# A delta-rule layer with a rational feed-forward on one core: the denominator's product on GpSimd, chunk scalars on VectorE, and a new written-out order

## The chip, the cores and the metric

The kernel runs on one core of a Trainium2 chip. A core has TensorE (PE; its weight loads are shown apart as PEld), VectorE (DVE), ScalarE (ACT), GpSimd (POOL) and SyncE (SP, which here only issues transfers). Each engine works through its own list of instructions in order and waits on semaphores. The metric is the device time of one execution in microseconds (us), the median of several.

## The reference

Two parts follow each other. The first is a delta-rule recurrence for each of 4 x 8 heads over 768 time steps with head size 48; the second is a feed-forward layer over the 3072 tokens with a rational function between two matrix products (384 to 2048 to 384).

```python
k_n = k / (np.linalg.norm(k, axis=-1, keepdims=True) + 1e-06)
for t in range(S):
    y[:, :, t] = einsum('bhd,bhde->bhe', q[:, :, t], state)
    v_old = einsum('bhde,bhd->bhe', state, kt)
    state = state + bt[..., None, None] * einsum('bhd,bhe->bhde', kt, vt - v_old)
x = y.transpose(0, 2, 1, 3).reshape(B * S, H * D)
h = x @ w_in
P = a[0] + a[1] * h + a[2] * h * h + a[3] * h * h * h
Q = 1.0 + abs(b[0]) * abs(h) + abs(b[1]) * h * h
out = (P / (Q + 1e-06)) @ w_out
```

`w_in` and `w_out` arrive as 64-bit floats; everything else is 32-bit.

## The kernel before

The sequence is cut into 12 chunks of 64 steps. Within a chunk the recurrence is solved with matrix products: keys are normalized and transposed, their products make a triangular system whose 16x16 blocks are inverted on VectorE (`inverse`), and the rest is solved in four rounds that go from TensorE to ScalarE and VectorE and back (`solve`). State and outputs follow. This is called the delta work below. Values are held as a pair of 16-bit halves, so each product is three passes of matmuls.

The feed-forward of a chunk has 256 tokens and is cut into 8 units of 256 hidden features, so there are 96 units. A unit is 18 matmuls into `ph` (`hidden`, L864), the rational function on 128x512 values, and 12 matmuls that add to `po` (`accumulate`, L931). The rational function: `numerator` makes z = |ph * B1| (ScalarE, L884), u = A3 * ph + a2 (ScalarE, L885), w = (z + B0) * ph (VectorE, L888) and |w| (ScalarE, L890). `cubic` makes u into the numerator but for its constant (VectorE, L896 and L898). `quotient` takes Ln and Exp of the denominator (ScalarE, L904 and L906), makes the first half of the result (VectorE, L910), a correction (VectorE, L913 and L915; L913 writes into the `ph` of the next unit) and its product with r (GpSimd, L917). The 128x512 buffers `mx` rotate over three, `ph` over two.

Each chunk needs factors that scale its 8 units: `scalar_steps` works them out on values of one column (128x1) with 14 calls of a small helper `affine` on ScalarE (L815), around three reciprocals on VectorE. It is called 13 times, twice for the first chunk (half of the weights each). `scales` makes the factors of queries and values with four small operations on ScalarE (L655 to L658), and `scaled` multiplies the queries by theirs on GpSimd (L228). At the start, block-diagonal buffers are set to zero (L185), the weights are brought in and split into halves, and the delta work of the first chunks runs beside it.

Nothing is left to a scheduler: `PLACES` gives every step of every stage (a step ends at a `yield`) a place in one order of 2996 places, and each engine gets its instructions in that order. Units of one chunk are interleaved with delta work of a later chunk; four units are under way at once, as a rule. After the last delta work only units are left.

Of the kernel before, what the change touches and what calls it, by code (L numbers as in the profile page):

```python
# [11 lines left out]
F32 = mybir.dt.float32  # L12
BF16 = mybir.dt.bfloat16
U32 = mybir.dt.uint32
AF = mybir.ActivationFunctionType
# [21 lines left out]
def kernel(  # L37
# [12 lines left out]
    nc = tc.nc  # L50
# [67 lines left out]
    coef = cpool.tile([P, 12], F32, name="coef")  # L118
    bblk = cpool.tile([P, NCH, 16], F32, name="bblk")
# [11 lines left out]
    def constants(_):  # L131
# [7 lines left out]
        for t in wide.values():  # L139
            nc.vector.memset(t[:, :, :, D:], 0.0)  # L140
        nc.gpsimd.memset(consts[:, 0:1], -15.0 * LN2)
# [23 lines left out]
        nc.scalar.activation(coef[:, 6:12], coef[:, 0:6], AF.Abs)  # L165
        nc.gpsimd.tensor_scalar(bblk, bblk, 1.0 / 256.0, 0.0, op0=ALU.mult, op1=ALU.add)

    filled = {}

    def zeros(nm):  # L170
        def stage(i):
# [8 lines left out]
            if nm == "rows":  # L180
                t = kn_b[i][:, :, :, :, D:DP]
            else:
                t = wt_b[i] if nm == "wt" else diag[nm][i]
            eng = nc.vector if nm in ("k", "w", "e", "rows") else nc.gpsimd
# [45 lines left out]
    def total(src, n, nm, pool=ps_f, tag="a"):  # L230
        pf = pool.tile([P, NPAIR * 512 if pool is ps_f else n], F32, tag=tag, name="pf" + nm)[:, :n]
        nc.tensor.matmul(pf, ones, src, start=True, stop=True)
        return pf
# [18 lines left out]
    NU = NF // 2  # L252
    GROUPS = ((0, NU // 2), (NU // 2, NU))
# [10 lines left out]
    def tables(g):  # L264
# [19 lines left out]
        pt = total(io, hi - lo, f"o{lo}", ps_f, "a")  # L284
# [347 lines left out]
    def scales(c):  # L632
# [31 lines left out]
    def queries_transposed(c):  # L664
        d = info[c]
        qt = d["qt"]
        scaled(qt[..., :D], d["sq"])
# [134 lines left out]
    def scalar_steps(c, lo=0, hi=NU):  # L802
# [7 lines left out]
        gm, rk, ikap, hm, top_, low, one, lin = (kp[:, i : i + 1] for i in range(8))  # L810
# [3 lines left out]
        def affine(dst, x, by, plus=0.0):  # L814
            nc.scalar.activation(dst, x, AF.Identity, scale=by, bias=plus)  # L815
# [8 lines left out]
        nc.vector.reciprocal(kp[:, 5:7], kp[:, 5:7])  # L824
        yield
        affine(lin, hm, m1)
        affine(top_, top_, hm)
        affine(top_, top_, hm)
        affine(lin, lin, one, m0)
        affine(gm, top_, low, lin)  # L830
# [9 lines left out]
        affine(ikap, rk, rk)  # L840
        affine(sf[:, 1:2], rk, rk)
        affine(sf[:, 3:4], sf[:, 2:3], ikap)
        affine(sf[:, 4:6], sf[:, 2:4], sf[:, 2:3])
# [7 lines left out]
    unit = {}  # L851
# [4 lines left out]
    def hidden(n):  # L856
        c, f2 = divmod(n, NU)
        x = toks[c]["x"]
        ph = ps_h.tile([P, 2, TG], F32, tag="h", name=f"ph_{n}")
# [12 lines left out]
        unit[n] = {"ph": ph}  # L872

    def numerator(n):
# [3 lines left out]
        A3, B1, A1, B0, A0, Q0 = (toks[c]["m"][:, i, f2 : f2 + 1] for i in range(6))  # L878
        ph = d["ph"]

# [3 lines left out]
        nc.scalar.activation(z, ph, AF.Abs, scale=B1)  # L884
# [15 lines left out]
    def quotient(n):  # L900
# [16 lines left out]
        nc.gpsimd.tensor_mul(g[:, 1], u, r)  # L917

    def accumulate(n):
# [26 lines left out]
        for p in PAIRS:  # L946
            if lo == 0:
# [5 lines left out]
        if hi == NU:  # L953
            yield
            for b in range(2):
                dst = out[2 * b * S : (2 * b + 2) * S].rearrange("(p t) e -> t p e", p=NPAIR)
                nc.sync.dma_start(out=dst[c * C : (c + 1) * C], in_=ob[b * C : (b + 1) * C])
# [4 lines left out]
        "zero_img": (  # L962
            (0, 76),
        ),
        "weights_in": (
# [981 lines left out]
```

## Time and profile before

| | |
|---|---|
| median of 3 runs | 764.49 us (762.56 to 769.67) |
| profiled execution | 765.28 us, span 763.6 us |
| busy in the span | DVE 691.9 us (91%), ACT 661.1 (87%), PE 629.3 (82%), POOL 311.7 (41%) |
| mean granted TensorE clock | 0.939 of full speed |
| moved by DMA | 84.35 MB |

The span runs from the first to the last instruction; the execution's time is 1.7 us more. Busy shares are averages: the kernel has a stretch in which weights come in and the first chunks are worked, a long stretch of units and delta work side by side, and an end with units alone. A matmul's end is modelled, so that a group of matmuls that stands alone counts with some tail that a group with a follower doesn't have.

### The profile page before, as it was taken

Reading aid. Unit: us, or ns where it says so; the run is one execution under the profiler, and the core shown is the slowest. Engines: PE = TensorE matmul, PEld = TensorE weight load, DVE = VectorE, ACT = ScalarE, POOL = GpSimd, SP = SyncE. Lnnn points to the kernel's source line nnn. Section 1 sums busy time; section 2 is a strip of 40 time slices with the busy share of each in tenths; the row PEclk is TensorE's granted clock in tenths of the full one; section 3 lists DMA queues with packets and bytes.
Section 4 is the critical chain, followed back from the end, with each engine's and each line's share of the span. In section 5 each row is a group of like instructions: output and inputs, shape, how many; then the busy total and the mean of one; then the engine's idle time right before and its main releaser. Section 6 shows DMA issues by size and latency. Waiting matters only on the chain.

```text
span 763.6 us, 23465 instructions
## 1 busy us (share of the span) xinstructions
PE 629.3 (82%) x9520; PEld 506.6 (66%) x9520; DVE 691.9 (91%) x1288; ACT 661.1 (87%) x1301; POOL 311.7 (41%) x321
## 2 busy tenths in 40 slices
PE   1321455886898999898998999999989999999986
PEld 1221455675677788686776787787778877777753
DVE  6789988867898999898998999999989999999995
ACT  4685998978898999798997999999989996899883
POOL 6742262533344265154342463354542432323222
PEclk9955786999799999899999999999999999999999
DMA  9699999778737675678464777685755832600000
GB/s 215 194 213 196 191 174 149 119 130 129 134 73 124 88 117 98 109 124 127 89 115 81 131 118 119 108 131 87 139 81 103 138 58 36 109 1 23 1 21 22
DMA packets 358412, 84.35 MB, mean 110 GB/s; under 512 B 349856, under 2 KB 352928, under 8 KB 358304
## 3 DMA queue, kind: packets, MB, share of 16 engines
q1 hardware_dynamic: 356128, 81.69, 61.0%
q8 instruction: 75, 1.23, 0.7%
q10 hardware_dynamic: 2176, 1.17, 0.5%
q14 instruction: 33, 0.27, 0.1%
HBM read 34.70 MB, written 13.65 MB: 63 GB/s over the span
## 4 chain that ended last, share of the span: by engine, by line
DVE 32%; ACT 25%; PE 20%; DMA 10%; issue 5%; SPq 3%; POOL 2%; ACTq 0%; DVEq 0%; POOLq 0%
PE ph L864 7%; PE po L931 5%; DVE mx L888 3%; ACT mx L885 3%; DVE ph L913 3%; ACT mx L884 3%; DVE mx L915 3%; DVE mx L896 3%; DVE mg L910 3%; DVE mx L898 3%; ACT kp L815 2%; DVE w_out L311 2%; PE pu L396 2%; ACT mx L904 2%; ACT mx L890 2%
## 5 line engine op out<-in xcount | busy, mean ns | idle before, releaser
L917 POOL TENSOR_TENSOR mg<-mx 128x512 f16<-128x512 f32 x96 | 129.7, 1351 | 277.2 <-DVE mx L915 167.5
L931 PE MATMUL po<-w_out,mg 128*128 128x384 f16 x1152 | 214.5, 329 | 4.3 <-POOL mg L917 2.4
L864 PE MATMUL ph<-xT,w_in 128*128 128x256 f16 x1728 | 205.1, 273 | 10.9 <-DVE mx L915 9.3
L864 PEld LDWEIGHTS <-w_in 128*128 128x128 f16 x1728 | 165.6, 98 | 41.0 <-DVE mx L915 9.3
L931 PEld LDWEIGHTS <-mg 128*128 128x128 f16 x1152 | 109.5, 99 | 65.8 <-POOL mg L917 3.1
L910 DVE SCALAR_TENSOR_TENSOR mg<-mx,msc 128x512 f16<-128x512 f32 x96 | 73.3, 764 | 2.7 <-ACT mx L906 2.6
L884 ACT ACTIVATE mx<-ph,msc 128x512 f32<-128x512 f32 x96 | 65.2, 679 | 12.0 <-PE ph L864 10.1
L913 DVE SCALAR_TENSOR_TENSOR ph<-mx,msc,mg 128x512 f32<-128x512 f32 x96 | 73.7, 768 | 1.5
L885 ACT ACTIVATE mx<-ph,coef,msc 128x512 f32<-128x512 f32 x96 | 74.1, 772 | 0.0
L888 DVE SCALAR_TENSOR_TENSOR mx<-mx,msc,ph 128x512 f32<-128x512 f32 x96 | 70.7, 737 | 1.9 <-issue 1.1
L915 DVE SCALAR_TENSOR_TENSOR mx<-mx,msc,ph 128x512 f32<-128x512 f32 x96 | 71.1, 741 | 1.3
L898 DVE SCALAR_TENSOR_TENSOR mx<-mx,msc,ph 128x512 f32<-128x512 f32 x96 | 70.8, 738 | 0.7
L904 ACT ACTIVATE mx<-mx,msc 128x512 f32<-128x512 f32 x96 | 69.3, 722 | 1.1
L890 ACT ACTIVATE mx<-mx 128x512 f32<-128x512 f32 x96 | 60.3, 628 | 10.7 <-DVE mx L888 10.4
L396 PEld LDWEIGHTS <-kbd 128*128 128x128 f16 x1680 | 57.6, 102 | 16.9 <-DVE sw L328 7.3
L896 DVE TENSOR_TENSOR mx<-ph,mx 128x512 f32<-128x512 f32 x96 | 65.4, 681 | 0.4 <-issue 0.2
L396 PEld LDWEIGHTS <-ebd 128*128 128x128 f16 x1728 | 51.2, 98 | 15.6 <-issue 11.4
L396 PE MATMUL pu<-z,ebd 128*128 128x48 f16 x1728 | 52.0, 186 | 11.4 <-DVE z L217 10.1
L906 ACT ACTIVATE mx<-mx 128x512 f32<-128x512 f32 x96 | 60.1, 628 | 1.1
L396 PEld LDWEIGHTS <-wbd 128*128 128x128 f16 x1152 | 33.2, 98 | 40.4 <-issue 38.7
L213 POOL TENSOR_TENSOR mm<-m,mm 128x512 f16<-128x512 f32 x24 | 31.6, 1328 | 34.4 <-ACT mm L207 28.1
L217 DVE SCALAR_TENSOR_TENSOR z<-pu,zmask,z 128x768 f16<-128x768 f32 x36 | 36.4, 1011 | 5.7 <-ACT z L215 5.7
(196 smaller groups left out, 1194.0 us busy)
## 6 DMA issues: line engine op xcount, KB each, us to landing
wsi<-in_moe_w_in_dram SPq DMA_DIRECT2D x8, 768.0 KB, 6.5
wso<-in_moe_w_out_dram SPq DMA_DIRECT2D x8, 768.0 KB, 6.5
gd<-g SPq DMA_DIRECT2D x24, 256.0 KB, 4.6
mbd<-mm SPq DMA_DIRECT2D x24, 256.0 KB, 5.3
wc<-img SPq DMA_DIRECT2D x24, 256.0 KB, 5.1
wbd<-wc SPq DMA_DIRECT2D x24, 256.0 KB, 5.0
knbd<-kn SPq DMA_DIRECT2D x44, 128.0 KB, 4.1
kw<-in_k_dram SPq DMA_DIRECT2D x48, 96.0 KB, 3.3
```

The source lines that it names most:

```text
L396: nc.tensor.matmul(dst[p][:, h], head(bd, lp, p * H + h), head(rt, rp, p * H + h), start=start and n == 0 and h == 0, stop=stop and n == l ...
L864: nc.tensor.matmul(ph[:, i], w_in[:, f2, wp, cc, i * P : (i + 1) * P], x[:, xp, cc], start=k == 0, stop=k == 3 * NCC - 1,)
L884: nc.scalar.activation(z, ph, AF.Abs, scale=B1)
L885: nc.scalar.activation(u, ph, AF.Identity, scale=A3, bias=a2)
L888: nc.vector.scalar_tensor_tensor(out=w, in0=z, scalar=B0, in1=ph, op0=ALU.add, op1=ALU.mult)
L896: nc.vector.tensor_mul(u, ph, u)
L898: nc.vector.scalar_tensor_tensor(out=u, in0=u, scalar=A1, in1=ph, op0=ALU.add, op1=ALU.mult)
L910: nc.vector.scalar_tensor_tensor(out=g[:, 0], in0=u, scalar=A0, in1=r, op0=ALU.add, op1=ALU.mult)
L913: nc.vector.scalar_tensor_tensor(out=t, in0=w, scalar=Q0, in1=g[:, 0], op0=ALU.add, op1=ALU.mult)
L915: nc.vector.scalar_tensor_tensor(out=u, in0=u, scalar=A0, in1=t, op0=ALU.add, op1=ALU.subtract)
L917: nc.gpsimd.tensor_mul(g[:, 1], u, r)
L931: nc.tensor.matmul(po[p], g[:, gp, i, p * P : (p + 1) * P], w_out[:, f2, wp, i], start=f2 == lo and i == 0 and k == 0, stop=f2 == hi - 1 a ...
```

## The change

For all units but the last two, |w| is made in another way: z = |ph| (a constant scale in place of a per-partition one), then w = B1 * z + B0 on ScalarE with scale and bias by partition, then w = w * z on GpSimd. VectorE's L888 and ScalarE's L890 fall away there. `hidden` and `numerator` have one more `yield` each, so there are 3188 places.

`scalar_steps` goes to VectorE: one operation on five columns makes five of the factors, and nine more operations do the rest. Three of the four small operations of `scales` are left, on VectorE. The queries' scale goes from GpSimd to ScalarE. The four zero fills of `kbd` (two), `wbd` and `ebd` go from VectorE to ScalarE. The `ph` of the last four units are put in banks of two other pools; the last two units' last product is on VectorE in place of GpSimd; of the very last output one half is copied by VectorE and its transfer is issued from ScalarE's queue. Every place in `PLACES` is new.

```diff
     def numerator(n):
-        nc.scalar.activation(z, ph, AF.Abs, scale=B1)
+        on_pool = f2 in POOL_UNITS and n < NCH * NU - 2
+        nc.scalar.activation(z, ph, AF.Abs, scale=1.0 if on_pool else col(1))
+        yield
         nc.scalar.activation(u, ph, AF.Identity, scale=A3, bias=a2)
         yield
-        nc.vector.scalar_tensor_tensor(out=w, in0=z, scalar=B0, in1=ph, op0=ALU.add, op1=ALU.mult)
-        yield
-        nc.scalar.activation(w, w, AF.Abs)
+        if on_pool:
+            nc.scalar.activation(w, z, AF.Identity, scale=B1, bias=B0)
+            yield
+            nc.gpsimd.tensor_mul(w, w, z)
+        else:
...
     def hidden(n):
-        ph = ps_h.tile([P, 2, TG], F32, tag="h", name=f"ph_{n}")
+        if n < N - 4:
+            ph = ps_h.tile([P, 2, TG], F32, tag="h", name=f"ph_{n}")
+        else:
+            if n % 2 == 0:
+                last[0] = (ps_f if n == N - 4 else ps_c).tile([P, 2, 2, TG], F32, tag="a", name=f"ph_{n}")
+            ph = last[0][:, n % 2]
...
+            if i == 0:
+                yield
     def quotient(n):
-        nc.gpsimd.tensor_mul(g[:, 1], u, r)
+        (nc.gpsimd if n < NCH * NU - 2 else nc.vector).tensor_mul(g[:, 1], u, r)
     def scalar_steps(c, lo=0, hi=NU):
-        affine(hm, wn, gm)
-        affine(top_, hm, m3, m2)
-        affine(low, hm, b1, b0)
-        affine(one, hm, b0, 1.0)
-        affine(low, low, hm, 1.0)
...
+        nc.vector.tensor_mul(hm, wn, gm)
+        nc.vector.scalar_tensor_tensor(out=kp[:, 4:9], in0=coef[:, 7:12], scalar=hm, in1=plus, op0=mult, op1=add)
+        nc.vector.tensor_scalar(low, low, hm, 1.0, op0=mult, op1=add)
...
+        nc.vector.tensor_scalar(top_, top_, hm, hm, op0=mult, op1=mult)
+        nc.vector.tensor_scalar(lin, lin, one, m0, op0=mult, op1=add)
+        nc.vector.scalar_tensor_tensor(out=gm, in0=top_, scalar=low, in1=lin, op0=mult, op1=add)
...
+        nc.vector.tensor_mul(ikap, rk, rk)
+        nc.vector.tensor_mul(sf[:, 1:2], rk, rk)
+        nc.vector.tensor_mul(sf[:, 3:4], sf[:, 2:3], ikap)
+        nc.vector.tensor_scalar_mul(sf[:, 4:6], sf[:, 2:4], sf[:, 2:3])
     def scales(c):
-        nc.scalar.copy(sc[:, 4:5], sc[:, 3:4])
-        nc.scalar.activation(sc[:, 6:7], sc[:, 3:4], AF.Copy, scale=1.0 / 16.0)
-        nc.scalar.activation(sc[:, 5:6], sc[:, 2:3], AF.Copy, scale=sc[:, 6:7])
-        nc.scalar.activation(sc[:, 6:7], sc[:, 3:4], AF.Copy, scale=1.0 / 256.0)
+        nc.vector.tensor_scalar(sc[:, 5:6], sc[:, 3:4], sc[:, 2:3], 1.0 / 16.0, op0=ALU.mult, op1=ALU.mult)
+        nc.vector.tensor_scalar_mul(sc[:, 6:7], sc[:, 3:4], 1.0 / 256.0)
+        nc.vector.tensor_copy(sc[:, 4:5], sc[:, 3:4])
     def queries_transposed(c):
-        scaled(qt[..., :D], d["sq"])
+        nc.scalar.activation(qt[..., :D], qt[..., :D], AF.Copy, scale=d["sq"])
     def zeros(nm):
+            if nm in ('k', 'w', 'e'):
+                whole = t.bitcast(F32).rearrange(FLAT[nm])
+                nc.scalar.activation(whole, consts[:, 0:1].broadcast_to(list(whole.shape)), AF.Copy, scale=0.0)
     def accumulate(n):
+            if p and n == N - 1:
+                nc.vector.tensor_scalar_mul(ob[:, p], po[p], ikap)
...
+                queue = nc.scalar if b and n == N - 1 else nc.sync
+                queue.dma_start(out=dst[c * C : (c + 1) * C], in_=ob[b * C : (b + 1) * C])
     PLACES = {
...
```

## Rows read from the trace of the kernel before

**Rows 1.** Busy time by stretch of the span (stretch in us, its length, then for each engine the busy us and in brackets the instructions; then the mean granted TensorE clock, the DMA engines' share and GB/s).

```profile
0.00:200.00 200.00, 98.92 (x1751) 84.10 (x1752) 163.07 (x338) 156.94 (x327) 88.38 (x110) 0.80 0.88 170
200.00:250.00 50.00, 46.93 (x669) 37.32 (x666) 46.49 (x89) 46.40 (x95) 23.46 (x25) 0.97 0.62 106
250.00:700.00 450.00, 430.06 (x6723) 348.05 (x6721) 428.30 (x777) 412.92 (x800) 181.57 (x173) 0.99 0.59 98
700.00:750.00 50.00, 47.00 (x350) 33.73 (x350) 49.29 (x81) 42.59 (x81) 15.36 (x12) 1.00 0.04 9
...
sum 764.00, PE 629.31 PEld 506.64 DVE 691.90 ACT 661.13 POOL 311.74; mean PE 125.86 PEld 101.33 DVE 138.38 ACT 132.23 POOL 62.35
```

The engines in it stand in the order PE, PEld, DVE, ACT, POOL.

**Rows 2.** The page's chain of work that ended last: shares of the span by engine.

```profile
DVE 32%; ACT 25%; PE 20%; DMA 10%; issue 5%; SPq 3%; POOL 2%; ACTq 0%; DVEq 0%; POOLq 0%
```

**Rows 3.** The second matrix product alone (L931) in the long stretch and in the end: PE busy us with the number of matmuls, 12 of which make a unit.

```profile
250.00:700.00 450.00, 155.59 (x834) 78.49 (x832) 0.99 0.59 98
700.00:750.00 50.00, 25.02 (x144) 14.01 (x144) 1.00 0.04 9
```

**Rows 4.** Groups of instructions by line, each shape apart: VectorE's six operations of a unit (count | busy us, mean ns of one | idle before them and who ended it).

```profile
L888 DVE SCALAR_TENSOR_TENSOR mx<-mx,msc,ph 128x512 f32<-128x512 f32 x96 | 70.7, 737 | 1.9 <-issue 1.1 <-ACT mx L885 0.7
L896 DVE TENSOR_TENSOR mx<-ph,mx 128x512 f32<-128x512 f32 x96 | 65.4, 681 | 0.4 <-issue 0.2
L898 DVE SCALAR_TENSOR_TENSOR mx<-mx,msc,ph 128x512 f32<-128x512 f32 x96 | 70.8, 738 | 0.7
L910 DVE SCALAR_TENSOR_TENSOR mg<-mx,msc 128x512 f16<-128x512 f32 x96 | 73.3, 764 | 2.7 <-ACT mx L906 2.6
L913 DVE SCALAR_TENSOR_TENSOR ph<-mx,msc,mg 128x512 f32<-128x512 f32 x96 | 73.7, 768 | 1.5
L915 DVE SCALAR_TENSOR_TENSOR mx<-mx,msc,ph 128x512 f32<-128x512 f32 x96 | 71.1, 741 | 1.3
```

**Rows 5.** The same view: ScalarE's five operations of a unit. L890 and L906 take no factor by partition, L904 takes one, L884 one (from PSUM), L885 two (from PSUM).

```profile
L884 ACT ACTIVATE mx<-ph,msc 128x512 f32<-128x512 f32 x96 | 65.2, 679 | 12.0 <-PE ph L864 10.1 <-DVE msc L847 0.7 <-DVE mg L910 0.5
L885 ACT ACTIVATE mx<-ph,coef,msc 128x512 f32<-128x512 f32 x96 | 74.1, 772 | 0.0
L890 ACT ACTIVATE mx<-mx 128x512 f32<-128x512 f32 x96 | 60.3, 628 | 10.7 <-DVE mx L888 10.4
L904 ACT ACTIVATE mx<-mx,msc 128x512 f32<-128x512 f32 x96 | 69.3, 722 | 1.1
L906 ACT ACTIVATE mx<-mx 128x512 f32<-128x512 f32 x96 | 60.1, 628 | 1.1
```

**Rows 6.** The same view: GpSimd's product of a unit.

```profile
L917 POOL TENSOR_TENSOR mg<-mx 128x512 f16<-128x512 f32 x96 | 129.7, 1351 | 277.2 <-DVE mx L915 167.5 <-ACT mx L904 18.4 <-PE pu L396 10.5
```

**Rows 7.** All of the helper `affine` (L815) over the whole span: ACT busy us and count.

```profile
0.00:764.00 764.00, 48.08 (x182) 0.94 0.62 110
```

**Rows 8.** Groups by line: small operations of one to four columns, on ScalarE (two of the four in `scales`) and on VectorE (one and two factors by partition).

```profile
L655 ACT COPY sc<-sc 128x1 f32<-128x1 f32 x12 | 2.3, 188 | 0.6 <-DVE sc L236 0.6
L657 ACT ACTIVATE sc<-sc 128x1 f32<-128x1 f32 x12 | 3.5, 295 | 0.4
L648 DVE TENSOR_SCALAR sc<-sc,sc 128x1 f32<-128x1 f32 x11 | 2.4, 214 | 0.4
L274 DVE TENSOR_SCALAR tab<-tab,coef 128x4 f32<-128x4 f32 x2 | 0.5, 246 | 0.1
```

**Rows 9.** Groups by line: the zero fills that move, the queries' scale, and a ScalarE operation of the scale's size with one factor by partition.

```profile
L185 DVE MEMSET kbd<- 128x2048 f32 x2 | 3.5, 1765 | 0.8 <-issue 0.8
L185 DVE MEMSET wbd<- 128x2048 f32 x1 | 1.8, 1765 | 1.3 <-PEq L1933 1.3
L185 DVE MEMSET ebd<- 128x2048 f32 x1 | 1.8, 1765 | 0.4 <-issue 0.4
L228 POOL TENSOR_SCALAR qw<-qw,sc 128x768 f32<-128x768 f32 x12 | 12.3, 1023 | 18.4 <-DVE sc L236 14.4 <-DMA wc<-img 3.2 <-DVE msc L847 0.6
L215 ACT ACTIVATE sh<-S,sc 128x768 f16<-128x768 f32 x11 | 10.2, 929 | 0.0
```

**Rows 10.** The chain in order of time in a part of the long stretch (start us, us, what): a unit's two matrix products with matmuls ahead of them and behind.

```profile
322.24 1.95 PE po L931 x12
...
325.40 1.97 PE ph L864 x18
```

**Rows 11.** Instructions in order of time near the end (start us, us, engine, line).

```profile
709.55 2.13 PE L864 MATMUL ph<-xT,w_in 128*128 128x256 f16 x18
709.63 1.28 POOL L917 TENSOR_TENSOR mg<-mx 128x512 f16<-128x512 f32 x1 [3.16 <-DVE mx L915]
...
710.65 0.81 DVE L910 SCALAR_TENSOR_TENSOR mg<-mx,msc 128x512 f16<-128x512 f32 x1
```

**Rows 12.** Instructions in order of time in the long stretch.

```profile
344.34 1.52 DVE L913 SCALAR_TENSOR_TENSOR ph<-mx,msc,mg 128x512 f32<-128x512 f32 x1
344.38 0.93 POOL L213 TENSOR_TENSOR rr<-v,rr 128x384 f16<-128x384 f32 x1 [1.55 <-ACT rr L207]
```

**Rows 13.** Instructions in order of time at the very end.

```profile
753.46 2.97 POOL L917 TENSOR_TENSOR mg<-mx 128x512 f16<-128x512 f32 x2 [3.48 <-DVE mx L915]
...
757.90 1.05 ACT L948 ACTIVATE ob<-po,kp 128x384 f32<-128x384 f32 x2 [6.65 <-PE po L931]
758.98 1.25 SPq L957 DMA_DIRECT2D out_dram<-ob  x2
```

More of the change, by code (lines that the diff above doesn't have):

```diff
@@ L848, in scalar_steps @@
         d["ikap"][lo] = hi, ikap
-    unit = {}
+    N = NCH * NU
+    unit, last = {}, {}
     acc = {}
@@ new lines @@
+            (805, 822),
+            (1090, 1098),
+            (1329, 1356),
+            (1535, 1567),
+            (1802, 1825),
+            (2027, 2091),
+            (2278, 2320),
+            (2541, 2580),
+            (2736, 2748),
+        ),
+        "hidden": (
+            (397, 439),
+            (412, 414),
+            (454, 465),
+            (536, 537),
+            (566, 579),
+            (632, 647),
+            (663, 669),
+            (709, 710),
+            (732, 737),
+            (754, 758),
+            (781, 782),
+            (797, 799),
+            (847, 848),
+            (874, 881),
+            (913, 918),
+            (937, 945),
+            (977, 978),
+            (1003, 1004),
+            (1040, 1041),
+            (1059, 1071),
+            (1086, 1087),
+            (1111, 1112),
+            (1140, 1141),
+            (1180, 1185),
+            (1206, 1220),
+            (1256, 1257),
+            (1260, 1263),
+            (1306, 1307),
+            (1338, 1344),
+            (1374, 1376),
+            (1405, 1406),
+            (1437, 1438),
+            (1471, 1478),
+            (1494, 1498),
+            (1524, 1527),
+            (1551, 1557),
+            (1582, 1594),
+            (1597, 1617),
+            (1643, 1644),
+            (1685, 1686),
+            (1709, 1718),
+            (1738, 1739),
+            (1760, 1761),
+            (1790, 1810),
+            (1817, 1826),
+            (1853, 1868),
+            (1901, 1902),
+            (1933, 1938),
+            (1963, 1964),
+            (1996, 1997),
+            (2017, 2029),
+            (2045, 2050),
+            (2080, 2081),
+            (2110, 2115),
+            (2125, 2139),
+            (2168, 2169),
+            (2197, 2214),
+            (2218, 2222),
+            (2255, 2270),
+            (2296, 2298),
+            (2315, 2316),
+            (2345, 2346),
+            (2372, 2378),
+            (2393, 2397),
+            (2429, 2430),
+            (2463, 2464),
+            (2488, 2500),
+            (2513, 2521),
+            (2534, 2543),
+            (2562, 2565),
+            (2593, 2595),
+            (2622, 2625),
+            (2675, 2682),
+            (2694, 2695),
+            (2712, 2713),
+            (2737, 2738),
+            (2762, 2772),
+            (2778, 2789),
+            (2813, 2820),
+            (2831, 2837),
+            (2857, 2859),
+            (2875, 2882),
+            (2899, 2903),
+            (2920, 2922),
+            (2932, 2933),
+            (2950, 2956),
+            (2986, 2987),
+            (3002, 3005),
+            (3030, 3032),
+            (3047, 3048),
+            (3056, 3058),
+            (3086, 3087),
+            (3053, 3098),
+            (3100, 3103),
+            (3126, 3129),
+            (3132, 3135),
+        ),
```

1474 lines of the change are left out of this document (685 added, 789 removed), and 177 rows, old and new, of tables (FLAT, PLACES).

## The prediction

> **What bounds the kernel now.** I read busy time by stretch first [rows 1], because the kernel has stretches with different limits. In the first 200 us no engine is near full: PE 98.9 of 200, DVE 163.1, ACT 156.9, with DMA at 0.88. From 250 to 700 us three engines are nearly full at once: PE 430.1 of 450 (95.6%), DVE 428.3 (95.2%), ACT 412.9 (91.8%); POOL has 181.6 (40%). From 700 to 750 us, with almost no delta work left, it is DVE: 49.3 of 50 (98.6%). The chain of waits says the same, being spread over DVE 32%, ACT 25% and PE 20% [rows 2]: no one engine holds it. The long stretch counts 834 / 12 = 69.5 units, 6.47 us each, or 8.7 chunks of 51.8 us; the end counts 144 / 12 = 12 units in 50 us, 4.17 us each [rows 3]. So relieving DVE alone gains in the long stretch only until PE is the limit, and PE's work isn't touched.
>
> **The change part by part, in the long stretch.**
>
> The denominator. DVE loses L888: 69.5 x 0.737 = 51.2 us [rows 4]. ACT loses L890 (0.628) and gets an operation from SBUF with two factors by partition, which no row shows. One factor costs L904 - L906 = 94 ns, so I take 628 + 2 x 94 = 816 ns; the bounds are 722 (one factor, L904) and 772 + 94 = 866. The z operation loses its factor: 679 - 94 = 585 ns. Net 816 - 628 - 94 = +94 ns a unit, 6.5 us in the stretch [rows 5]. POOL gets a product of 128x512 with 32-bit output. The nearest row, L917, has the same shape with 16-bit output: 1.35 us [rows 6]; I take that, with 0.93 (a shorter product, [rows 12]) and 2.7 (twice L917) as ends. That is 69.5 x 1.35 = 93.8 us.
>
> The chunk scalars. ACT loses 48.1 / 13 = 3.7 us a chunk [rows 7] and four operations of 188 to 295 ns, 0.9 us [rows 8]: 8.7 x 4.6 = 40 us. DVE gets 10 and 3 operations of one to five columns at 0.15 to 0.25, I take 0.2 (214 for one column, 246 for four, less some overlap) [rows 8]: 2.6 us a chunk, 22.6 us.
>
> The queries' scale. POOL loses 1.02 us a chunk, ACT gets 0.93 (its row of that size with one factor) [rows 9]: -8.9 and +8.1 us.
>
> Sums for the 450 us: DVE 428.3 - 51.2 + 22.6 = 399.7 (89%); ACT 412.9 + 6.5 - 40 + 8.1 = 387.5 (86%); POOL 181.6 + 93.8 - 8.9 = 266.5 (59%); PE stays at 430.1 (96%). **PE becomes the limit.** How full can a limiting engine be? DVE reached 98.6% in the end [rows 1], but with simpler work. At 98.6% PE would need 436 us (-14), at today's 95.6% 450 (0). A part of PE's busy time is the modelled tail of groups that stand alone: 18 matmuls of `hidden` count 2.13 us alone [rows 11] and 1.97 with a follower [rows 10]. A denser PE sheds some of that: if each unit's 18 did, 69.5 x 0.16 = 11 us more, which makes the far end -25. I take PE at 97.5% (441) with a third of the 11 us shed: -13 us. The 50 us before it (PE 46.9, DVE 46.5) go the same way: -1.5.
>
> The first 200 us. Four fills leave DVE, 4 x 1.765 = 7.1 us, for ACT, where I reckon 1.87 each (628 ns for 512 elements, and (929 - 722) / 256 = 0.81 ns for each further one) [rows 5, 9]. ACT has 43 us of room, DVE 37. If all four were on the path it would be -7, if they now hold up ACT's own path +7.5. The order of the delta work and the transfers is new and not to be read from rows; I take -2 with those ends.
>
> The end. A unit takes 4.17 us at DVE's pace (sum of the six: 4.43, less overlap). Without L888 DVE has 3.5, and PE's 1.97 + 1.95 = 3.92 [rows 10] is next. At 4.0 the 12 units give -2; the ends are 0 and -3. The last four units' own banks take away a wait of `hidden` for the `ph` two units before, which PE's pace covers anyway: nothing. Behind the last unit: the last products on DVE take 0.76 in place of GpSimd's 2.97 for two, of which PE waits for some 0.8; two output copies side by side, 1.05 to 0.6; two issues on two queues, 1.25 to 0.6 [rows 13]: -1.9.
>
> Sum: -2 - 1.5 - 13 - 2 - 1.9 = -20.4, from a span of 763.6 to 743.2; the execution's time lies 1.7 above it, 744.9, and the profiled execution lay 0.8 above the median of the runs shown: **744 us**, -2.7%.
>
> **What is queued behind the new waits.** Ln (L904) now waits for GpSimd's product, and behind it in ACT's list stand Exp and the next units' z and u, on which PE's second product and `ph`'s release hang. On GpSimd the product stands among the delta work's halves and L917.
>
> **The rivals.**
>
> *Ln waits for GpSimd (slower).* Before, ACT waited 10.7 us in all for DVE at L890 and 1.1 at L904 [rows 5]. ACT will have 450 - 387.5 = 62.5 us of room in the stretch, 0.90 us a unit. If Ln stands on average more than 0.90 us idle for a product of 1.35 us or more, ACT's list becomes the pace. With 1.2 us it is 0.3 x 78 units (from 200 us on) = +23, and -4 from the end: 783 us. For it: GpSimd rises to 59% in order, and its products are the longest step of a unit. Against it: four units are under way, so that the Ln of one can be placed behind work of others, and POOL's idle time before L917 is mostly for L915, not for its own queue [rows 6]. 0.13.
>
> *The two engines slow each other (no gain).* L910 took 0.81 while a GpSimd product ran [rows 11] against a mean of 0.764, and one L913 1.52 beside a GpSimd subtraction [rows 12] against 0.768 [rows 4]. DVE will have 450 - 399.7 = 50.3 us of room, 30.4 more than PE; over two operations of 69.5 units that is 0.22 us each. Only if the mean delay passes 0.22 us does DVE set the pace again; at 0.3 it takes most of the gain in the long stretch: 757 us. The one pair at 0.05 speaks against it, as 0.05 x 139 = 7 us stays in DVE's room. The Trainium skill, GPSIMD Engine Reference, Specifications, has a rule that speaks for it: GpSimd's SBUF interfaces are shared with VectorE, and there is contention with VectorE instructions that have two SBUF inputs; L910 and L913 are such, the four others read PSUM too. The two pairs agree that such delays occur, not that they are frequent. 0.06.
>
> *PE doesn't get fuller (no gain).* Delta work is a row of hand-overs between engines and may keep PE at 95.6% whatever room DVE has. Then only -2, -2 and -1.9 are left: 758 us. For it: PE and DVE are both at 95% now and it isn't shown which waits for which. 0.09.
>
> *PE has more room than its busy time shows (much faster).* Then the long stretch follows the mean load of DVE and ACT, which falls by 7 and 6%: 500 x 0.065 = -32, with -6 elsewhere: 727 us and below. The tail of 0.16 us per group [rows 10, 11] is the sign for it. The Trainium skill, Perfetto Trace Analysis, Identifying the Most-Contended Engine, says that matmul busy time is a bad measure of how near TensorE is to its limit, and that weight-load busy time is better. By that rule PE would have room here and this rival would be the likelier. The trace: weight loads are busy 348.1 of 450 us, 77% [rows 1]. Against the rival: 1.97 + 1.95 us for a unit's matmuls in a row [rows 10] is a floor that no measure of busy time lowers. 0.12.
>
> **How the numbers follow.** My forecast (730 to 756) has 0.60, the slower case 0.13, the two without gain 0.15, the much faster 0.12. A difference of under 1% can't be told from none here: 1% is 756.8 and 772.1. Faster: 0.60 + 0.12 = 0.72; within 1%: 0.15; slower: 0.13. The range that leaves out some 0.07 below and 0.13 above is 726 to 766.
>
> **What would show it.** Right: from 250 us on PE at 97% or more and DVE under 92%; the 18 matmuls of `hidden` nearer 1.97 than 2.13; 69.5 units in some 437 us; in the end about 4.0 us a unit with PE as the chain; the two-factor operation at 816 ns, the new product at 1.35 us; L904's idle time small. Wrong: idle time before L904 ended by GpSimd above 60 us in all; L910 and L913 above 0.95 us in the mean; PE idle with DVE and ACT idle too; or a first unit that ends much later than before, in which case the new order of the first 200 us decides and not the engines' loads.

## The result and the profile after

The changed kernel takes 769.39 us (median of 20 runs, 766.44 to 774.01) against 764.36 us of the kernel before on the same chip (20 runs): ratio 1.0065 [1.0045, 1.0085]. It is 0.65% slower, within the 1% that the prediction counted as no change, and outside its range of 726 to 766 us. The profiled execution took 773.27 us, 4 us above the median, with a span of 771.2 us against 763.6.

The page's busy times, and busy time by stretch (the columns of [rows 1]):

```profile
PE 634.9 (82%) x9520; PEld 510.3 (66%) x9520; DVE 696.7 (90%) x1359; ACT 636.5 (83%) x1088; POOL 429.6 (56%) x403
...
0.00:200.00 200.00, 107.38 (x1683) 88.23 (x1684) 160.97 (x361) 159.52 (x291) 93.61 (x117) 0.77 0.83 165
250.00:700.00 450.00, 419.05 (x6603) 340.30 (x6601) 428.26 (x804) 384.41 (x646) 270.80 (x234) 0.99 0.60 98
700.00:750.00 50.00, 47.67 (x429) 36.06 (x425) 44.56 (x78) 40.35 (x67) 30.44 (x23) 1.00 0.04 9
```

In the long stretch ScalarE and GpSimd came out as forecast (384 and 271 us, against 387.5 and 266.5). VectorE did not: it was to fall to 399.7 us and stands at 428.26, what it was before. TensorE, which was to become the limit, fell from 430 to 419. Over the whole span VectorE rose by 4.8 us [rows 1], although 94 instructions of L888, 69 us, are gone from it.

The operations themselves have the prices forecast. Groups by line, each shape apart (columns as in [rows 4]):

```profile
L913 POOL TENSOR_TENSOR mx<-mx 128x512 f32<-128x512 f32 x94 | 127.7, 1359 | 130.3 <-ACT mx L911 125.0 <-ACT lgq L257 2.7 <-DVE mx L923 0.7
L911 ACT ACTIVATE mx<-mx,msc 128x512 f32<-128x512 f32 x94 | 76.4, 813 | 0.0
L931 ACT ACTIVATE mx<-mx,msc 128x512 f32<-128x512 f32 x96 | 69.1, 719 | 12.2 <-POOL mx L913 11.8
L937 DVE SCALAR_TENSOR_TENSOR mg<-mx,msc 128x512 f16<-128x512 f32 x96 | 77.3, 806 | 2.5 <-ACT mx L933 1.7 <-PE po L958 0.5
L940 DVE SCALAR_TENSOR_TENSOR ph<-mx,msc,mg 128x512 f32<-128x512 f32 x96 | 85.0, 886 | 2.9 <-ACT mx L907 0.2
L839 DVE SCALAR_TENSOR_TENSOR kp<-kp 128x1 f32<-128x1 f32 x13 | 6.8, 522 | 0.5
L852 DVE TENSOR_SCALAR sf<-sf 128x2 f32<-128x2 f32 x13 | 6.4, 491 | 0.5
L841 DVE TENSOR_SCALAR kp<-kp,top 128x1 f32<-128x1 f32 x13 | 2.7, 207 | 0.1
```

The product took 1.36 us, the two-factor operation 0.81, and Ln (now L931) stood 12 us in all, as much as L890 and L904 together before (11.8 us) [rows 5]. What grew is the busy time of VectorE's own instructions. L937 and L940, the old L910 and L913 [rows 4], rose by 42 and 118 ns in the mean. An operation on one column, L839, has a mean of 522 ns, and L841, of the same size, 207. The instructions of these two lines over the whole span (minimum, median and maximum in ns, first and last start) show that this is not the operation's price:

```profile
L839 DVE SCALAR_TENSOR_TENSOR kp<-kp x13: 218/381/1334, 123.9 to 713.8; 128x1 f32<-128x1 f32 x13
...
L841 DVE TENSOR_SCALAR kp<-kp,top x13: 200/207/214, 125.7 to 717.3; 128x1 f32<-128x1 f32 x13
```

The instructions in order of time show what a long one stands for:

```profile
500.73 1.28 POOL L944 TENSOR_TENSOR mg<-mx 128x512 f16<-128x512 f32 x1
...
501.05 1.01 DVE L584 TENSOR_TENSOR pr<-wt,ab 128x36 f32<-128x36 f32 x1
```

L584 multiplies 36 columns. It starts while GpSimd's product runs and ends at 502.06, just behind the product's end at 502.01. In a record of busy time this looks like work, and it is a wait.

To size it I took, within each group of the same line and shape, the time that the shortest fifth of its instructions stays at or below as the price, and summed what the longer ones took above it (those over 1.15 times the price plus 60 ns). I call this VectorE's **standing time**; it is worked out from all of the trace's VectorE instructions and stands in no single row. Before it is 14.7 us in 27 instructions, after 61.2 us in 106; every one of the 133 overlaps a running GpSimd instruction. Of the 46.5 us more, 17.5 are in the chunk scalars on VectorE, 16.5 in L937 and L940, most of the rest in the delta work. By place: 200 to 700 us went from 2.8 to 40.3.

Two more counts over the whole trace say that this is a wait and not chance. Of the 106 instructions, 98 end a fixed time behind the GpSimd instruction that they started under: their price less 0.12 to 0.21 us. So what a meeting costs is what is left of GpSimd's instruction, less those 0.12 to 0.21 us. And of the 466 VectorE instructions that start with more than 0.3 us of a GpSimd instruction to go, 96 have two tensor inputs from SBUF, or are a `TENSOR_SCALAR` over two columns or more from SBUF: 92 of these stand. Of the other 370 none does.

The ledger of VectorE, an estimate from these prices: 691.9 - 69 (L888) - 7 (fills) + some 34 (scalars at unhindered prices) + 2 (last units) = 652. Measured is 696.7; the 46.5 us of standing time fill the gap.

About half of the loss comes at the end. In the two profiled executions, which lie 8 us apart where the medians lie 5 apart, unit 92's second product ends 4.0 us later than before (754.4 against 750.4 us) and the last unit's 8.3 us later (766.3 against 758.0). Instructions in order of time:

```profile
749.03 5.36 PE L958 MATMUL po<-w_out,mg 128*128 128x384 f16 x32
755.19 1.48 PE L958 MATMUL po<-w_out,mg 128*128 128x384 f16 x8 [0.79 <-DVE mg L937]
759.86 6.40 PE L958 MATMUL po<-w_out,mg 128*128 128x384 f16 x28 [3.19 <-POOL mg L944]
```

All `hidden` work is done by 749.2 us, and then TensorE waits for `mg`, 3.19 us in one place. VectorE works until 765.4 us.

### The profile page after: what moved, and what is told of

Same layout as the page of the kernel before. It is cut to its first block, busy times and chain, and to the rows that moved or that the text cites. A ratio compares the mean times of both kernels' runs of the same rounds, so it can differ in the third digit from the quotient of the medians.

```text
span 771.2 us, 23426 instructions
## 1 busy us (share of the span) xinstructions
PE 634.9 (82%) x9520; PEld 510.3 (66%) x9520; DVE 696.7 (90%) x1359; ACT 636.5 (83%) x1088; POOL 429.6 (56%) x403
## 3 DMA queue, kind: packets, MB, share of 16 engines
q10 hardware_dynamic: 2320, 1.36, 0.6%
## 5 line engine op out<-in xcount | busy, mean ns | idle before, releaser
L881 PE MATMUL ph<-xT,w_in 128*128 128x256 f16 x1728 | 214.2, 277 | 17.4 <-DVE mx L942 14.0
L913 POOL TENSOR_TENSOR mx<-mx 128x512 f32<-128x512 f32 x94 | 127.7, 1359 | 130.3 <-ACT mx L911 125.0
L940 DVE SCALAR_TENSOR_TENSOR ph<-mx,msc,mg 128x512 f32<-128x512 f32 x96 | 85.0, 886 | 2.9 <-ACT mx L907 0.2
L937 DVE SCALAR_TENSOR_TENSOR mg<-mx,msc 128x512 f16<-128x512 f32 x96 | 77.3, 806 | 2.5 <-ACT mx L933 1.7
L931 ACT ACTIVATE mx<-mx,msc 128x512 f32<-128x512 f32 x96 | 69.1, 719 | 12.2 <-POOL mx L913 11.8
L911 ACT ACTIVATE mx<-mx,msc 128x512 f32<-128x512 f32 x94 | 76.4, 813 | 0.0
L904 ACT ACTIVATE mx<-ph 128x512 f32<-128x512 f32 x94 | 55.6, 592 | 22.7 <-PE ph L881 20.0
L925 DVE SCALAR_TENSOR_TENSOR mx<-mx,msc,ph 128x512 f32<-128x512 f32 x96 | 71.1, 741 | 2.3 <-ACT mx L904 0.9
L942 DVE SCALAR_TENSOR_TENSOR mx<-mx,msc,ph 128x512 f32<-128x512 f32 x96 | 71.2, 741 | 1.3
L923 DVE TENSOR_TENSOR mx<-ph,mx 128x512 f32<-128x512 f32 x96 | 65.4, 681 | 6.2 <-ACT mx L907 3.6
L412 PEld LDWEIGHTS <-kbd 128*128 128x128 f16 x1680 | 57.3, 101 | 12.0 <-issue 10.2
L933 ACT ACTIVATE mx<-mx 128x512 f32<-128x512 f32 x96 | 60.0, 628 | 1.7
L412 PE MATMUL pu<-z,ebd 128*128 128x48 f16 x1728 | 50.8, 185 | 10.2 <-DVE z L232 9.9
L322 POOL TENSOR_SCALAR w_out<-w_out 128x768 f32<-128x768 f32 x15 | 15.4, 1029 | 50.9 <-ACT w_out L320 47.3
L412 PE MATMUL pe<-wc,wbd 128*128 128x48 f16 x576 | 17.2, 187 | 26.1 <-DMA wc<-img 25.9
```

The source lines that it names most:

```text
L412: nc.tensor.matmul(dst[p][:, h], head(bd, lp, p * H + h), head(rt, rp, p * H + h), start=start and n == 0 and h == 0, stop=stop and n == l ...
L881: nc.tensor.matmul(ph[:, i], w_in[:, f2, wp, cc, i * P : (i + 1) * P], x[:, xp, cc], start=k == 0, stop=k == 3 * NCC - 1,)
L911: nc.scalar.activation(w, z, AF.Identity, scale=B1, bias=B0)
L913: nc.gpsimd.tensor_mul(w, w, z)
L923: nc.vector.tensor_mul(u, ph, u)
L925: nc.vector.scalar_tensor_tensor(out=u, in0=u, scalar=A1, in1=ph, op0=ALU.add, op1=ALU.mult)
```

## The experiments

Each ratio is to the kernel before on the same chip; the changed kernel stands at 1.0065. Spans and busy times are of the profiled execution, and the standing time is worked out as above. My theory ahead of the runs: VectorE still sets the pace, and its standing beside GpSimd took back what L888 gave. Rivals: the wait of Ln for the product, the new order, and TensorE.

**The product.** First GpSimd's product is left out, then it writes a buffer that nobody reads, then VectorE does it.

```diff
-            nc.gpsimd.tensor_mul(w, w, z)
# e1: nothing
# e2:
+            idle = sb.tile([P, 2, TG], F32, tag="idle", name=f"idle{n}", bufs=1)
+            nc.gpsimd.tensor_mul(idle, w, z)
# e3:
+            nc.vector.tensor_mul(w, w, z)
```

> The changed kernel without GpSimd's new product: w stays B1 * |ph| + B0 (the product with |ph| is left out), all else and the order as it is. Theory A, the two engines: a VectorE instruction with two SBUF inputs stands until GpSimd's running instruction ends; summed over groups, VectorE's instructions took 61 us more than the shortest fifth of their own group in the changed kernel and 15 us before. Then that excess falls to 20 us or less, VectorE's busy time to 645 to 665 us, and the time to 740 to 755. Theory B, Ln waits for GpSimd's product: the same fall of time, but the excess stays above 45 us. Theory C, the new order by itself costs it: 764 to 772 us as now.

> The changed kernel with GpSimd's product written to a spare buffer that nobody reads, so that Ln waits for ScalarE's own w alone (the product doesn't enter the result). Theory A: the excess of VectorE's instructions stays at 50 to 70 us and the time at 762 to 772. Theory B: the time falls to 740 to 755 as without the product. Theory C: 764 to 772.

> The changed kernel with the same product on VectorE in place of GpSimd, order as it is. Theory A: 94 products of 0.68 to 0.75 us come back to VectorE (+66) and some 40 us of excess go; VectorE is the limit and the time is 780 to 795. If GpSimd's product cost VectorE nothing (my prediction): +66 us on VectorE and nothing back, 800 or more. Theory C: says nothing of it beyond the load.

| run | median us | ratio | span | DVE busy | standing |
|---|---|---|---|---|---|
| e1_product_left_out | 756.19 | 0.9877 [0.9853, 0.9901] | 754.7 | 682.1 | 46.1 |
| e2_product_unread | 764.75 | 1.0013 [0.9990, 1.0036] | 761.2 | 690.0 | 55.0 |
| e3_product_on_vectore | 833.38 | 1.0906 [1.0867, 1.0946] | 837.6 | 749.1 | 58.9 |

Without the product the time falls by 14 us (0.0188 of 764), so the product with all that waits for it costs that much. But the kernel is then only 9 us faster than before, and the standing time falls only to 46.1 us, where I expected 20 or less. That was a miss: most of it is due to GpSimd's other instructions. GpSimd is busy 306.0 us in e1 and 311.7 before, so with the same load VectorE stands three times as long. What differs is where VectorE's two-input operations stand in the order, and the scalars among them (10.8 of the 46.1 us).

e2 was to part the wait for the product from its presence, and it doesn't. Ln reads `w`, but it writes `r`, which is the `z` that the product still reads; so Ln waits for GpSimd as before. Group by line of e2 (L932 is Ln, L914 the product):

```profile
L932 ACT ACTIVATE mx<-mx,msc 128x512 f32<-128x512 f32 x96 | 69.0, 719 | 11.6 <-POOL idle L914 11.2
```

Its 4 us less than the changed kernel come with 6 us less of standing time and with Ln's wait as it was; why it stands less is open. So e1's 14 us hold both the wait of Ln and the standing beside the product. That Ln's wait isn't what holds the time is seen in e5, e10 and e16 below, where it grows while the time falls.

In the third run the loss is far larger than I expected: on VectorE the product takes 804 ns, and Ln stands 60.6 us (58.7 of it for VectorE). In these places GpSimd is the better one for it. As a test between the theories the run tells nothing: 800 us or more was to speak for the prediction, but the standing time, of which 40 us were to go by my theory, hardly moved, and Ln's new wait alone is nearly the whole loss against the changed kernel (64 us).

**The order.** Before's forms in the new order (what is changed back beside the product: scalars, `scales`, fills, queries' scale), and the other way round, the product in the old order, without and with the scalars on VectorE.

```diff
# e4, against the changed kernel
-        on_pool = f2 in POOL_UNITS and n < NCH * NU - 2
+        on_pool = False
# e7 and e8, against the kernel before
+        on_pool = n < NCH * NU - 2
+        if on_pool:
+            nc.scalar.activation(w, z, AF.Identity, scale=B1, bias=B0)
+            yield
+            nc.gpsimd.tensor_mul(w, w, z)
+        else:
...
```

> The new order (and the new banks and end) with the operations and engines of before: |w| by VectorE and ScalarE, chunk scalars and the four small operations on ScalarE, the queries' scale on GpSimd, fills on VectorE; the few units whose first step stands ahead of their scalars get one more ScalarE operation. Theory C: slower than the changed kernel or as slow, 769 or more, though the engines' loads are those of before. Theory A: the order was made for other loads, so some loss, but the excess of VectorE's instructions is back at 15 to 20 us and the time is 760 to 775, near the kernel before.

> The kernel before, in its own order, with the product alone: |ph|, B1 * z + B0 on ScalarE and the product on GpSimd for all but the last two units. VectorE 692 - 69 = 623 plus new waits (10 to 20), ScalarE 661 + 9 = 670. Theory D: VectorE is no longer the pace, 740 to 755. Theory E: an order made for other operations costs whatever the loads are, 765 to 800.

> The run before this one and the chunk scalars on VectorE as in the change (scales and queries as before). VectorE + 33 and some 15 of waits, about 680; ScalarE - 48, about 622. Theory D: 750 to 765. Theory E: 765 to 800.

e4_order_alone: 909.38 us, 1.1896 [1.1858, 1.1934], DVE busy 712.7, standing 28.2. It is inconclusive. With L888's form in the new order VectorE stands idle 90.3 us ahead of that operation (before 1.9) and ScalarE 48.2 us ahead of |w| (before 10.7), waits that neither kernel has; in two units the operation even reads `ph` behind the previous unit's correction to it. The order alone was not tried in another way.

e7_old_order_product: 838.89 us, 1.0981 [1.0945, 1.1016], span 837.3; e8_old_order_product_scalars: 845.40 us, 1.1087 [1.1033, 1.1142]. Both lie far above what any theory gave them, 800 us at most. Standing time is 79.6 and 78.1. Groups by line of e7_old_order_product (L910 is Ln, L885 the z operation, L892 the product, L923 the last product):

```profile
L892 POOL TENSOR_TENSOR mx<-mx 128x512 f32<-128x512 f32 x94 | 127.5, 1357 | 144.0 <-ACT mx L890 106.4 <-DVE mx L902 14.7 <-DVE mg L916 6.8
L910 ACT ACTIVATE mx<-mx,msc 128x512 f32<-128x512 f32 x96 | 69.3, 721 | 42.3 <-POOL mx L892 42.1
L885 ACT ACTIVATE mx<-ph 128x512 f32<-128x512 f32 x94 | 55.3, 588 | 36.4 <-POOL mg L923 18.3 <-PE ph L864 17.6 <-POOL mx L892 0.2
```

Here the wait of the prediction's rival is real: Ln stands 42 us for GpSimd, z another 18. VectorE is busy 437.5 of the 500 us from 200 to 700 against 476.6 in the changed kernel. In the new places Ln waits 12 us. With the old ones the product costs 75 us over the kernel before, and with the scalars on VectorE 82; the whole change with its new places costs 5. How much of the 75 is Ln's and z's wait and how much standing time, 65 us more than before, no run parts.

**The shape and place of the small operations.** In e5 each operation of the scalars with two tensors or several columns becomes one to three with one column and factors by partition, and a two-column step of `scales` becomes two (the cut shows a part); in e6 the scalars are back on ScalarE; in e10 both GpSimd products go in halves.

```diff
# e5, e16
-        nc.vector.scalar_tensor_tensor(out=kp[:, 4:9], in0=coef[:, 7:12], scalar=hm, in1=plus, op0=mult, op1=add)
+        nc.vector.tensor_scalar(top_, hm, m3, m2, op0=mult, op1=add)
+        nc.vector.tensor_scalar(one, hm, b0, 1.0, op0=mult, op1=add)
+        nc.vector.tensor_scalar(low, hm, b1, b0, op0=mult, op1=add)
...
-        nc.vector.tensor_mul(ikap, rk, rk)
+        nc.vector.tensor_scalar_mul(ikap, rk, rk)
...
# e6
-        nc.vector.tensor_mul(hm, wn, gm)
+        affine(hm, wn, gm)
...
# e10, e16
-            nc.gpsimd.tensor_mul(w, w, z)
+            for i in range(2):
+                nc.gpsimd.tensor_mul(w[:, i], w[:, i], z[:, i])
...
+        for i in range(2):
+            (nc.gpsimd if n < NCH * NU - 2 else nc.vector).tensor_mul(g[:, 1, i], u[:, i], r[:, i])
```

> The changed kernel with the chunk scalars on VectorE as before this run, but each as an operation of one column with one tensor input and its factors as scalar operands (no second tensor, no two columns); two more small operations a call, and the powers of two of scales as two of one column. In the changed kernel such operations showed no wait for GpSimd (237 and 263 ns in the mean, near their shortest fifth), while those with two tensors or two columns did (up to 1334). Theory D, VectorE's own time with its waits for GpSimd is still the pace: the excess falls from 61 to 40 to 45 us, VectorE's busy time to 680 to 685 and the time to 754 to 760. Theory E, the new order's hand-overs are the pace: the excess falls as well, the time stays at 764 to 770.

> The changed kernel with the chunk scalars back on ScalarE (14 small operations a call). VectorE loses some 33 us of them and their waits, to about 645; ScalarE goes from 636 to about 685. Theory D: 748 to 762. Theory E: the scalars take longer from hand-over to hand-over than the order was made for, 768 to 785.

> The changed kernel with both GpSimd products of a unit as two instructions of 256 columns each. GpSimd has some 25 to 30 us more in all, but no product lasts longer than 0.75 us, so that a VectorE instruction behind it stands for half as long. Theory A with D: the excess falls from 61 to 48 to 54 us and the time to 760 to 766. If a VectorE instruction is not let in between two GpSimd instructions in a row, excess and time stay or rise, 768 to 775.

| run | median us | ratio | span | DVE busy | standing |
|---|---|---|---|---|---|
| e5_scalars_one_column | 761.45 | 0.9969 [0.9943, 0.9996] | 762.0 | 686.0 | 38.2 |
| e6_scalars_on_scalare | 787.90 | 1.0312 [1.0277, 1.0346] | 786.7 | 662.1 | 42.6 |
| e10_products_in_halves | 762.49 | 0.9968 [0.9944, 0.9992] | 761.0 | 686.6 | 48.2 |

e5 shows that the form counts. There are 64 more VectorE instructions than in the changed kernel and 10.7 us less busy time, and the time falls by 7 us (1.0065 to 0.9969). The time is 1 us above the range of my theory, the standing time 2 below. Groups by line of e5 (L936 is Ln, L918 the product):

```profile
L842 DVE TENSOR_SCALAR kp<-kp,coef 128x1 f32<-128x1 f32 x13 | 2.8, 214 | 0.5
L853 DVE TENSOR_SCALAR kp<-kp 128x1 f32<-128x1 f32 x13 | 2.7, 207 | 0.1
L857 DVE TENSOR_SCALAR sf<-sf 128x1 f32<-128x1 f32 x13 | 2.7, 211 | 0.0
L936 ACT ACTIVATE mx<-mx,msc 128x512 f32<-128x512 f32 x96 | 69.1, 719 | 13.2 <-POOL mx L918 12.8
```

Standing time in the scalars falls from 17.5 to 0.5 us, and Ln waits no less than in the changed kernel. e6 takes more from VectorE than any other run, 35 us, and is 24 us slower than before. I read it as again an order that doesn't fit its operations, with the scalars coming late at ScalarE's places; no run shows that. In e10 GpSimd works 32 us longer (461.5) and VectorE stands 13 us less: half of that beside the new product (16.9 to 10.2 us), which ends sooner. Ln's wait for it grows to 17.8 us, and the time still falls by 7.

**Who sets the pace.** Half of one VectorE step of each unit (the cubic's second operation) is left out, in the changed kernel and in the one before; and 4 of the 12 matmuls of `accumulate` are, in both.

```diff
# e9, e15
-        nc.vector.scalar_tensor_tensor(out=u, in0=u, scalar=A1, in1=ph, op0=ALU.add, op1=ALU.mult)
+        nc.vector.scalar_tensor_tensor(out=u[:, 0], in0=u[:, 0], scalar=A1, in1=ph[:, 0], op0=ALU.add, op1=ALU.mult)
# e13, e14
-            for i in range(2):
+            for i in range(0 if k == 1 else 2):
```

> The changed kernel with the second operation of cubic on half of its columns (the other half of u misses A1 and the second product with h). No operation, wait or place is gone; VectorE alone has 96 x 0.27 to 0.35 = 26 to 34 us less. Theory D, VectorE with its waits for GpSimd is the pace: the time falls nearly as much, to 738 to 750. If TensorE is the pace, as predicted for the changed kernel: 764 to 769. Theory E, hand-overs at fixed places: in between, 750 to 764.

> The kernel before with the second operation of cubic on half of its columns (26 to 34 us less on VectorE), in its own order. If VectorE was its pace: 732 to 742. Theory E, as in the changed kernel, where the same gave 12 us: 748 to 757.

> The changed kernel without the second of the three passes of accumulate (4 of a unit's 12 matmuls, the low half of w_out, are left out); TensorE has 96 x 4 x 0.162 = 62 us less, no operation of another engine, no wait on another engine and no place is gone. My prediction's step 'TensorE becomes the limit': 62 us of TensorE would give nearly as much, 715 to 735. Theory D, VectorE with its waits is the pace: 764 to 770. Theory E, the pace is handed from engine to engine at fixed places, so that each engine's time counts in part: 745 to 762.

> The same left out of the kernel before (4 of 12 matmuls of accumulate), in its own order. My prediction took its long stretch as shared between TensorE, VectorE and ScalarE: then the 62 us give a part. Theory E: 740 to 758. If VectorE alone was the pace there: 760 to 766.

| run | median us | ratio | span | PE busy | DVE busy |
|---|---|---|---|---|---|
| e9_half_vector_step | 757.77 | 0.9908 [0.9877, 0.9939] | 754.5 | 632.4 | 675.5 |
| e15_half_vector_step_before | 755.17 | 0.9874 [0.9852, 0.9895] | 754.9 | 631.2 | 669.0 |
| e13_light_tensore | 766.75 | 1.0041 [1.0010, 1.0072] | 763.6 | 587.0 | 689.8 |
| e14_light_tensore_before | 768.00 | 1.0046 [1.0027, 1.0065] | 767.9 | 582.7 | 693.0 |

Busy time from 200 to 700 us, e13 (columns as in [rows 1]):

```profile
200.00:700.00 500.00, 438.85 (x7158) 360.01 (x7157) 474.95 (x914) 432.79 (x731) 307.34 (x266) 0.98 0.62 100
```

With 48 us less on TensorE the changed kernel gains 2 us (1.0065 to 1.0041, the intervals overlap), and the kernel before, with 47 us less, gains nothing: its ratio is above 1. VectorE stays at 475 of 500 us. With 21 and 23 us less on VectorE the two kernels gain 12 and 10 us. So TensorE is not the limit in either; VectorE is the nearest to it, and about half of what it is relieved of comes back. The TensorE runs fit theory D (e14 lies 2 us above its range), the VectorE runs theory E, so neither theory fits all. In e1, e5, e9, e10 and in the three runs below VectorE's busy time is 10 to 21 us under the changed kernel's, and the time 3 to 15 us. ScalarE was relieved in no run.

**Versions that might beat both.** e11 adds to e5 the product on GpSimd for the last two units as well; e12 adds e10's halves to that; e16 is e5 and e10 together.

```diff
# e11, e12
-        on_pool = f2 in POOL_UNITS and n < NCH * NU - 2
+        on_pool = f2 in POOL_UNITS
```

> The one-column scalars, and the denominator's product on GpSimd for the last two units too. In the changed kernel the last four units leave VectorE 2 x 5 + 2 x 7 operations of 0.67 us after their last matmul of hidden, and PE waits; with two fewer each for the last two, VectorE has 2.7 us less there. Expected: 1.5 to 3 us below the one-column run, 758 to 760. If the product's hand-over costs as much at the end: 761 to 763.

> One-column scalars, products in halves, and the product on GpSimd for all units: the version for both kernels to be beaten by. Theory A with D: 750 to 757. If the halves bring nothing: as the run before it, 758 to 760.

> One-column scalars and both GpSimd products in halves, the end as in the changed kernel. In the runs so far the span is VectorE's busy time, its waits for GpSimd included, and some 72 to 82 us. Theory D: the excess falls to 26 to 32 us, VectorE's busy time to 675 to 680, the time to 753 to 759, some 1% below the kernel before. If hand-overs hold it: 759 to 763, no better than the one-column run.

e11_one_column_end: 767.26 us, 1.0025 [0.9994, 1.0055]; e12_combined: 758.36 us, 0.9908 [0.9875, 0.9942]; e16_one_column_halves: **753.84 us, 0.9868 [0.9833, 0.9904]**, with 676.3 us of DVE and 27.0 of standing time. The end gained nothing by the product on GpSimd: by the ratios the kernels with it are 4 (e11 against e5) and 3 us (e12 against e16) above the ones without, with intervals that touch or overlap, and e11 lies above both of its forecasts. e16 beats both kernels, by 1.3% and 2.0%. Its time from 200 to 700 us, its last product, VectorE's L946 and Ln (L937):

```profile
200.00:700.00 500.00, 483.74 (x7515) 391.67 (x7511) 477.31 (x990) 444.57 (x748) 344.04 (x433) 1.00 0.62 101
...
L951 POOL TENSOR_TENSOR mg<-mx 128x256 f16<-128x256 f32 x188 | 146.4, 800 | 62.9 <-DVE mx L948 39.0 <-ACT mx L912 6.0 <-PE pu L412 5.5
L946 DVE SCALAR_TENSOR_TENSOR ph<-mx,msc,mg 128x512 f32<-128x512 f32 x96 | 80.8, 841 | 2.9 <-ACT mx L912 0.2
L937 ACT ACTIVATE mx<-mx,msc 128x512 f32<-128x512 f32 x96 | 69.1, 720 | 19.0 <-POOL mx L919 18.5
```

VectorE is as full as ever, 477 of 500 us, but 7515 matmuls fit into the stretch where the changed kernel has 7356. A half product takes 0.80 us where the whole took 1.39, and L946 (L940 before the edit) falls from 886 to 841 ns. Ln waits 18.5 us for the product, 7 more than in the changed kernel, while the time is 15 us lower: so it isn't Ln's wait that holds the time.

## Why the prediction was wrong

**The operations' prices: right.** The two-factor operation took 813 ns (816 forecast), the product 1359 (1350), the z operation 592 (585), the queries' scale 933 (929), a fill 1.90 us (1.87). L904's idle time (now L931's) is small, as the forecast case had it.

**"PE becomes the limit" failed.** It rested on VectorE's sum of 399.7 us, and on 95.6% of modelled busy time being near to full. The first didn't come: VectorE stands at 428.26. On the second, e13 and e14 show that TensorE held neither kernel at that share: 7% less of its busy time moves the time by 2 us or nothing. Whether it would have been the limit beside a VectorE of 399.7 us no run shows; in e16 it is busy 483.7 of 500 us (96.7%). The rule of the Trainium skill that the prediction weighed and set aside (Perfetto Trace Analysis, Identifying the Most-Contended Engine: matmul busy time is a bad measure of how near TensorE is to its limit) agrees with e13 and e14. The rival drawn from it, 727 us, still did not come, since VectorE was not relieved.

**"The one pair at 0.05 speaks against it, as 0.05 x 139 = 7 us stays in DVE's room" is the term that was mis-sized.** The standing time rose by 46.5 us, 37.5 of them from 200 to 700 us. The mechanism was the rival of the two engines, with 0.06. Three things were wrong in it. I let it count in L910 and L913 alone; they carry 16.5 us of it, and the rest is mostly in the chunk scalars and the delta work, because any VectorE operation with two inputs from SBUF can be caught. Its condition, a mean delay of over 0.22 us in those two, was not met (0.04 and 0.12) and not needed. And I took the 0.05 us of one pair as a typical size, against the 0.75 of the other.

Both pairs follow one rule, and the rows had it. L910 ends at 711.46 us and GpSimd's product beside it at 710.91 [rows 11]; L913 ends at 345.86 and GpSimd's subtraction at 345.31 [rows 12]. Each ends 0.55 us behind GpSimd; one had 0.26 us of GpSimd's instruction ahead of it, the other 0.97. In the trace of before, 39 instructions of L910 and L913 start beside a running GpSimd instruction. The 21 with more than 0.25 us of it to go are all longer than their price, by 0.07 us or more; for 19 of them it was under 0.3 us. So the delays were small before because of where the order put these operations, and the new places were not to be read from rows of before.

A page of the Trainium skill that I did not weigh says this of such a change: Perfetto Trace Analysis, Optimizing Scalar/DVE Operations, that GpSimd and VectorE share an SBUF port, so that moving work between the two might not help. The traces agree in part: of the 46.5 us, 15 go when the moved product is left out (e1), and the rest is met by GpSimd's other instructions.

**The signs of being wrong did not come up.** Idle time before Ln is 12.2 us (the sign was 60), L910 and L913 stand at 0.81 and 0.89 us (0.95), and the first unit ends 8.7 us later (155.1 us against 146.4) but the fifth 3.7 us earlier. The wait was spread over many operations that the signs did not watch.

**The small operations' 0.2 us: right as a price, wrong in place.** Unhindered they take 0.15 to 0.27 us, but the forms with two inputs or two columns had means of up to 0.52 (e5 gave it back).

**Ln's wait.** It did not come in the new order: 12.2 us in all, where before 1.1 stood at Ln and 10.7 at L890 [rows 5]. No run takes this wait away alone, but in e5, e10 and e16 it is larger (13.2, 18.1 and 19.0 us) and the time lower. e7 shows it whole: 42 us, and 838.89 us. The rival judged the order rightly as the thing that decides.

**The end: wrong sign.** The -2 and -1.9 came out as some 4 us more, from unit 92 to the last. TensorE is done with `hidden` 17 us ahead of its last matmul, against 11.5 before; VectorE's and ScalarE's steps of the last units are then left over together, with TensorE idle. "PE's 3.92 is next" overlooked that. That the other banks for `ph` cause it is likely and not shown.

**The first 200 us.** No difference that I can tell: unit 8 ends at 227.5 us against 228.9 before, unit 64 at 608.3 against 610.8. In between the difference goes both ways (unit 24 ends 5.8 us earlier, unit 56 4.5 us later). From unit 68 on the units are behind, by 5.3 us at unit 80 (705.3 us against 700.0).

**What stays open.** In kernels whose order was made for their operations the span is VectorE's busy time, standing included, plus 71 to 86 us, at 463 to 478 of the 500 us; that is a reading of the runs, not a law, and it does not say why only half of e9's relief came back. How much of the loss is the order's own, apart from standing time, would have needed a clean e4. And e16, with 27.0 us of standing time left, is at 753.84 us and not at the forecast 744: no run brought standing time back to the 14.7 us of before with the product on GpSimd.

## What to carry to other kernels

Before moving work from VectorE to GpSimd, find in the trace VectorE's operations that start beside a GpSimd instruction and are longer than their group's shortest ones, and see how much of that instruction was left: the busy share hides this wait. It hangs on the places more than on GpSimd's load: at the same load it was 14.7 us before and 46.1 in e1. Small operations on VectorE were safest here with one column and factors by partition, and in this kernel GpSimd's instructions were better short. A written order belongs to its operations: the product alone cost 75 us in the old order, the whole change 5 in its own.

## What was unexpected of the hardware

- A VectorE operation that starts under a running GpSimd instruction can stand until that one ends: 1.01 us for 36 columns, 1334 ns against 218 for one column. Those caught have two tensor inputs from SBUF, or two columns or more in a `TENSOR_SCALAR` from SBUF (L852, 491 ns in the mean): 92 of 96 that had over 0.3 us of GpSimd's instruction to go; one-column `TENSOR_SCALAR` operations (L841: 200 to 214 ns) and those with an input from PSUM (L942: 741 ns, as before) were not, with none of 370. The Trainium skill, GPSIMD Engine Reference, Specifications, names operations with two SBUF inputs, and those in a two-port mode; Trainium Architecture — The Big Picture, What this means for kernel authors, calls the shared port a lock and not a split of bandwidth. The traces agree with the first part and, by the L584 row and the 98 of 106 that end with GpSimd, with the lock. Whether those with two columns or more are in such a mode no run here shows.
- TensorE's granted clock fell at the very end of the changed kernel. Busy time by stretch (columns as in [rows 1]):

```profile
756.00:758.00 2.00, 0.66 (x5) 0.20 (x2) 1.86 (x4) 1.18 (x2) 0.00 (x0) 1.00 0.00 0
760.00:762.00 2.00, 2.00 (x7) 0.91 (x6) 1.93 (x4) 1.07 (x2) 0.00 (x0) 0.50 0.03 8
764.00:766.00 2.00, 1.96 (x13) 0.92 (x11) 1.34 (x2) 0.00 (x0) 0.00 (x0) 1.00 0.00 0
```

TensorE had waited from 756.7 to 759.9 us; then the clock is 0.50 (1.2 of 2.4 GHz), and 7 matmuls fit into 2 us in place of 13. The last `mg` on VectorE comes only at 765.4 us, so this cost little. Before, the clock was 1.00 from 745 us to the last matmul, where TensorE waited 1.63 us.
